# The first three blocks of a conv-and-MLP kernel in halves of 256 tokens, with the first convs mostly on TensorE

## The chip, the cores and the metric

The kernel runs on one core of one Trainium2 chip. The metric is device time in microseconds of one execution, lower is better; a time below is the median of several executions, with the lowest and highest where that matters. The changed kernel and each experiment ran on one chip together with runs of the kernel before, and are compared with those. All times that are compared are of fast runs (TensorE's mean granted clock 0.988 to 1.0); one execution in a slow state (0.563) is told apart from them. A few words used throughout: a **block** is 512 tokens of two batch rows; a **group** is the unit that the changed kernel works in, half a block or a whole one; the **first product** makes the 2048 hidden values from the conv's output, the **second product** brings them back to 192; **half clock** is said where matmuls took up to twice as long as the same ones elsewhere.

## The reference, cut to what matters

```python
# x (8, 4096, 192), weight (8 heads, 7 taps), w_in (192, 2048), w_out (2048, 192)
w = softmax(weight)                              # over the 7 taps
out[b, s, h, :] = sum_k w[h, k] * x_pad[b, s + k, h, :]     # causal conv, 6 zeros in front
h = out.reshape(32768, 192) @ w_in
y = maximum(0.01 * h, h) @ w_out                 # leaky ReLU between two products
```

## The kernel before

x is cast to bf16 and transposed by DMA, so that channels lie on partitions and tokens on the free axis (`xt`). The conv is 7 VectorE operations for each of 3 chunks of channels: one multiply and six multiply-adds (STT below) with the tap as a per-partition scalar. The first product reads the conv's result `yt`, ScalarE applies the leaky ReLU out of PSUM, and the second product of the block before is issued between the first product's steps.

```python
def conv_jobs(blk):                              # 3 chunks x 7 taps, 512 tokens each
    for c in range(NCH):
        for k in range(K):
            src = xt[rp][:, c, BASE + k + st * ST : BASE + k + (st + 1) * ST]
            # k == 0: tensor_scalar_mul(dst, src, wk[:, c, 0:1])
            # else:   scalar_tensor_tensor(out=dst, in0=src, scalar=wk[:, c, k:k+1], in1=dst, mult, add)
# ... the start
cast_first(0, 0, nc.vector.tensor_copy)
cast_first(0, 1, nc.scalar.copy)
transpose_x(0)                                   # DMA transposes, three of them
for job in conv_jobs(0):
    job()
# ... 40 matmuls that only warm TensorE up, then the loop:
for blk in range(NBLK + 1):
    jobs = conv_jobs(blk + 1) if blk + 1 < NBLK else []
    for j in range(STEPS):                       # 8 steps
        # mm1(blk, f) for two f: 12 matmuls of 512 columns, two ScalarE activations
        # mm2(n): 32 matmuls of 192 columns for the block before
        for job in jobs[3 * j : 3 * (j + 1)]:
            job()                                # next block's conv on VectorE
# ... cut: loads, softmax of the taps, output copies on VectorE
```

In the traces each engine ran its operations in the order of issue. That is what the argument below turns on: an operation that stood behind a wait waited too (VectorE's conv for 3.54 us behind one copy, under experiment 6).

## Time and profile before

| | kernel before |
|---|---|
| time, median | 715.68 us (715.51 to 715.94) |
| TensorE busy | 690.0 of 713.3 us |
| first useful matmul | 30.85 us (four of its twelve at 27.34) |
| a block in the middle | 20.93 us |
| block 4's first matmul | 109.93 us |

The lines behind this table stand in the prediction. How to read them: TensorE is busy for 97% of the span, so the middle can't get faster without less TensorE work. But the first 30.85 us hold next to no product, and the block after that has no second product to go with it. "Block 4's first matmul" is a milestone: from there on both kernels do the same, so a difference in that time is the whole difference.

### The profile page before, as it was taken

How to read it: one execution, taken by the hardware profiler on the slowest of the kernel's cores; microseconds unless marked ns; L12 is line 12 of the kernel's file. 1: busy time of each engine (PE TensorE's matmuls, PEld its weight loads, DVE VectorE, ACT ScalarE, POOL GpSimd, SP SyncE). 2: the span in 40 equal slices, each digit the busy share in tenths (PEclk: the TensorE clock that was granted, in tenths of full speed). 3: DMA queues.
4: the chain of work that ended last, by engine and by line, in shares of the span. 5: the costliest groups of instructions: out<-in, count | busy, mean ns of one | idle time of the engine just before them, and what ended most of it. 6: DMA issues, size and time to landing. Idle time of an engine off the chain costs nothing.

```text
span 713.3 us, 24704 instructions
## 1 busy us (share of the span) xinstructions
PE 690.0 (97%) x11166; PEld 593.0 (83%) x11166; DVE 535.6 (75%) x940; ACT 500.4 (70%) x518; POOL 142.0 (20%) x198
## 2 busy tenths in 40 slices
PE   2889999999999999999999999999999999999997
PEld 1347788888888888888888888888888888888887
DVE  2977877777787777788777778777777877777812
ACT  2197777777777777777777777777777777777770
POOL 7522201222210222220222222012222111000000
PEclk9999999999999999999999999999999999999999
DMA  9946435565545556653565654465556455133112
GB/s 198 152 26 79 73 77 67 76 85 79 90 66 78 75 67 90 80 75 73 79 76 73 90 81 73 74 72 76 79 80 89 66 84 72 43 69 57 46 36 67
DMA packets 188040, 55.08 MB, mean 77 GB/s; under 512 B 151584, under 2 KB 187936, under 8 KB 187936
## 3 DMA queue, kind: packets, MB, share of 16 engines
q0 software_dynamic: 98768, 14.17, 29.0%
q1 hardware_dynamic: 89152, 39.34, 24.0%
q8 instruction: 87, 1.43, 0.8%
q14 instruction: 17, 0.14, 0.1%
q10 hardware_dynamic: 16, 0.00, 0.0%
HBM read 29.88 MB, written 25.17 MB: 77 GB/s over the span
## 4 chain that ended last, share of the span: by engine, by line
PE 93%; DVE 2%; DMA 2%; ACT 2%; SPq 0%; issue 0%; DVEq 0%
PE po L248 48%; PE ph L230 45%; DVE yt L133 2%; ACT g L237 2%; DMA xt<-x_bf 1%; DMA x_nat<-in_x_dram 1%; SPq L83 0%; DVE yt L127 0%; DVE o_sb L290 0%; DVEq L127 0%
## 5 line engine op out<-in xcount | busy, mean ns | idle before, releaser
L237 ACT ACTIVATE g<-ph 128x1024 bf16<-128x1024 f32 x512 | 496.2, 1021 | 189.1 <-PE ph L230 189.1
L133 DVE SCALAR_TENSOR_TENSOR yt<-xt,wk,yt 128x512 bf16<-128x512 bf16 x576 | 431.4, 749 | 14.0
L248 PEld LDWEIGHTS <-g 64*128 64x128 bf16 (+1 forms) x8048 | 374.6, 94 | 32.7 <-issue 0.2
L230 PE MATMUL ph<-yt,w_in 64*128 64x512 bf16 x3072 | 393.8, 377 | 5.4 <-DVE yt L133 2.9
L248 PE MATMUL po<-w_out,g 64*128 64x192 bf16 (+1 forms) x8048 | 399.0, 243 | 0.0
L230 PEld LDWEIGHTS <-w_in 64*128 64x128 bf16 x3072 | 233.7, 94 | 62.8 <-issue 12.2
L74 POOL DMA_DIRECT2D x_bf<-in_x_dram x180 | 133.6, 765 | 447.4 <-DMA xt<-x_bf 437.2
L290 DVE COPY o_sb<-po 128x192 f32<-128x192 f32 x256 | 91.6, 358 | 146.6 <-PE po L248 143.9
L127 DVE TENSOR_SCALAR yt<-xt,wk 128x512 bf16<-128x512 bf16 x96 | 33.4, 348 | 9.2 <-DMA xt<-x_bf 9.2
L216 PE MATMUL warm<-xt,ident 128*128 128x512 bf16 x40 | 11.7, 466 | 10.2 <-DMA xt<-x_bf 10.2
L216 PEld LDWEIGHTS <-ident 128*128 128x128 bf16 x40 | 4.6, 115 | 16.9 <-issue 14.1
L91 ACT CAST x_bf<-x_nat 128x768 bf16<-128x768 f32 x3 | 2.5, 831 | 6.1 <-DMA x_nat<-in_x_dram 6.1
L190 PE MATMUL wps<-w,sel 8*128 8x7 f32 x6 | 1.4, 354 | 4.1 <-DVE w L187 4.1
L162 POOL DMA_DIRECT2D w_in<-in_moe_w_in_dram x8 | 5.1, 645 | 0.0
L190 PEld LDWEIGHTS wps<-w,sel 8*128 8x128 f32 x6 | 1.4, 321 | 4.0 <-issue 4.0
L170 ACT ACT_TABLE_LOAD x1 | 1.3, 1283 | 1.4 <-PEq L332 1.4
L167 POOL DMA_DIRECT2D w_out<-in_moe_w_out_dram x1 | 1.2, 1201 | 1.7 <-DMA w_in<-in_moe_w_in_dram 1.7
L196 DVE COPY wk<-wps 128x21 f32<-128x21 f32 x1 | 0.2, 181 | 1.6 <-PE wps L190 1.6
L152 POOL TENSOR_SCALAR_AFFINE_SELECT sel<-sel 8x384 f32<-8x384 f32 x2 | 1.1, 535 | 0.1
L175 DVE TENSOR_REDUCE nmax<-w 8x1 f32<-8x7 f32 x1 | 0.1, 148 | 1.2 <-DMA w<-in_weight_dram 1.2
L91 DVE CAST x_bf<-x_nat 128x768 bf16<-128x768 f32 x1 | 0.9, 941 | 0.0
L182 DVE TENSOR_REDUCE ssum<-w 8x1 f32<-8x7 f32 x1 | 0.1, 149 | 0.8 <-ACT w L179 0.8
(14 smaller groups left out, 2.7 us busy)
## 6 DMA issues: line engine op xcount, KB each, us to landing
out_dram<-o_sb SPq DMA_DIRECT2D x128, 192.0 KB, 2.1
x_bf<-in_x_dram POOLq DMA_DIRECT2D x180, 64.0 KB, 3.2
x_nat<-in_x_dram SPq DMA_DIRECT2D x4, 384.0 KB, 4.6
w_in<-in_moe_w_in_dram POOLq DMA_DIRECT2D x8, 192.0 KB, 8.7
xt<-x_bf SPq DMA_TRANSPOSE x96, 2.5
w_out<-in_moe_w_out_dram POOLq DMA_DIRECT2D x1, 768.0 KB, 15.9
w<-in_weight_dram ACTq DMA_DIRECT2D x1, 0.2 KB
```

Of the source, the lines that this page charges most:

```text
L74: nc.gpsimd.dma_start(out=t[:, c, :, e, :], in_=src[2 * rp + e, :, :, c * CH : (c + 1) * CH],)
L91: copy(out=x_bf[blk][:, :, :, e, :], in_=x_nat[blk][:, e, :, :].rearrange("p s (c k) -> p c s k", c=NCH),)
L127: lambda s=src, d=dst, c=c: nc.vector.tensor_scalar_mul(d, s, wk[:, c, 0:1])
L133: lambda s=src, d=dst, c=c, k=k: nc.vector.scalar_tensor_tensor(out=d, in0=s, scalar=wk[:, c, k : k + 1], in1=d, op0=mybir.AluOpType.mult, ...
L162: nc.gpsimd.dma_start(out=w_in[e * CH : (e + 1) * CH, :, fs], in_=moe_w_in[:, fs].rearrange("(c p) f -> p c f", p=CH),)
L170: nc.scalar.activation(out=junk, in_=junk, func=mybir.ActivationFunctionType.Exp)
L190: nc.tensor.matmul(out=wps[:, 0, c * K : (c + 1) * K], lhsT=sel[:, c, :, :].rearrange("h e k -> h (e k)"), rhs=w8, start=True, stop=True,)
L216: nc.tensor.matmul(out=wa[:, 0, :], lhsT=ident, rhs=xt[0][:, 0, HALO : HALO + ST], start=(i == 0), stop=(i == NWARM - 1),)
L230: nc.tensor.matmul(out=ph[:, e, :], lhsT=w_in[ps, c, f * 128 : (f + 1) * 128], rhs=y[ps, c, :], start=(c == 0), stop=(c == NCH - 1),)
L237: return nc.scalar.activation(out=g[blk][:, f, :, :], in_=ph, func=mybir.ActivationFunctionType.Prelu, alpha=0.01,)
L248: ins = nc.tensor.matmul(out=po[m], lhsT=g[b][ps, fc, e, s * 128 : (s + 1) * 128], rhs=w_out[ps, fc, :], start=(rt != 1 and fc == 0), stop ...
L290: nc.vector.tensor_copy(out=o_sb[:, n % 2, :], in_=po.pop(n))
```

## The change

It is meant to start the products sooner. The first three blocks are cut into halves of 256 tokens (groups 0 to 5; block 3, whole, is group 6). x of blocks 0 and 1 is transposed on TensorE, out of PSUM by VectorE and ScalarE. In groups 0 and 1 the conv of two of the three chunks is done by matmuls with diagonal matrices (one per tap, twice, as a tap is split into two bf16 parts). The output copies of the first three blocks move from VectorE to ScalarE.

```diff
+    NHALF = 3
+    NPEC = 2
+    groups = [(b, h * HT, HT) for b in range(NHALF) for h in range(2)]
+    groups += [(b, 0, ST) for b in range(NHALF, NBLK)]
...
+    def transpose_first(q):      # 12 nc.tensor.transpose of 64 x 128 into two PSUM tiles
+    def evac_first(q, *copies):  # the two copies into xt
+    def pe_conv_jobs(grp, c):    # 14 matmuls: lhsT=diag[c][:, p, k, :], rhs=xt shifted by k
...
-    transpose_x(0)
-    for job in conv_jobs(0):
-        job()
+    transpose_first(0)
+    warm(3)
+    evac_first(0, nc.vector.tensor_copy, nc.scalar.copy)
+    # diag[0] by 2 VectorE products, diag[1] by 14 ScalarE activations
+    # chunks 0, 1 by pe_conv_jobs, chunk 2 by conv_jobs
...
+        copy = nc.scalar.copy if b < NHALF else nc.vector.tensor_copy
...
+            if i in (1, 2) and j == 0:
+                transpose_first(i + 1)
+                evac_first(i + 1, nc.vector.tensor_copy, nc.vector.tensor_copy)
+            for job in ahead[per * j : per * (j + 1)]:
+                job()
+            if i == 1 and j == 3:
+                for e in range(2):
+                    cast_first(3, e, nc.vector.tensor_copy)
```

(Cut: loads in halves, the softmax's reciprocal after the matmul, the bookkeeping of second-product slots. `i` is the group, `j` its step; a half group has 4 steps, a whole one 8.)

More of the change, by code (lines that the diff above doesn't have):

```diff
@@ L38 @@
     SUB = ST // 128
+    HT = ST // 2
+    HS = SUB // 2
     NFC = F // 128
@@ L41 @@
     NBLK = (B // 2) * NB
-    STEPS = 2 * SUB
-    FPS = NFC // STEPS
     LAG = NFC + NFC // 2
-    LAST = (NBLK - 1) * STEPS - 1
     WQ = 4
+    NHALF = 3
+    NPEC = 2
     const_pool = ctx.enter_context(tc.tile_pool(name="const", bufs=1))
@@ L78, in load_x @@
         x_bf[blk] = t
-    def load_first(blk):
-        t = stage_pool.tile([128, 2, SUB, D], FP32, name="x_nat")
-        for e in range(2):
-            nc.sync.dma_start(
-                out=t[:, e, :, :],
-                in_=x[e, blk * ST : (blk + 1) * ST, :].rearrange("(c p) d -> p c d", p=128),
-            )
-        x_nat[blk] = t
-        x_bf[blk] = xb_pool.tile([128, NCH, SUB, 2, CH], BF16, name="x_bf")
-    def cast_first(blk, e, copy):
-        copy(
-            out=x_bf[blk][:, :, :, e, :],
-            in_=x_nat[blk][:, e, :, :].rearrange("p s (c k) -> p c s k", c=NCH),
-        )
     def transpose_x(blk):
@@ L101, in transpose_x @@
         if st == 0:
-            xt[rp] = xt_pool.tile([128, NCH, HALO + S], BF16, name="xt")
-            nc.vector.memset(xt[rp][:, :, 0:HALO], 0.0)
+            new_xt(rp)
         t = x_bf.pop(blk)
@@ L111, in transpose_x, with new_xt, load_first, cast_first @@
             )
+    def new_xt(rp):
+        xt[rp] = xt_pool.tile([128, NCH, HALO + S], BF16, name="xt")
+        nc.vector.memset(xt[rp][:, :, 0:HALO], 0.0)
+    def load_first(q):
+        t = stage_pool.tile([128, 2, HS, D], FP32, name="x_nat")
+        for e in range(2):
+            nc.sync.dma_start(
+                out=t[:, e, :, :],
+                in_=x[e, q * HT : (q + 1) * HT, :].rearrange("(c p) d -> p c d", p=128),
+            )
+        x_nat[q] = t
+    def cast_first(q, e, copy):
+        if q % 2 == 0 and e == 0:
+            x_bf[q // 2] = xb_pool.tile([128, NCH, SUB, 2, CH], BF16, name="x_bf")
+        h = q % 2
+        copy(
+            out=x_bf[q // 2][:, :, h * HS : (h + 1) * HS, e, :],
+            in_=x_nat[q][:, e, :, :].rearrange("p s (c k) -> p c s k", c=NCH),
+        )
@@ new lines @@
+    ptr = {}
+    def transpose_first(q):
+        ts = [
+            psum_o.tile([128, HS, NCH, CH], BF16, name=f"ptr{i}", tag="po") for i in range(2)
+        ]
+        for s in range(HS):
+            for c in range(NCH):
+                for i in range(2):
+                    ps = slice(i * CH, (i + 1) * CH)
+                    nc.tensor.transpose(
+                        out=ts[i][:, s, c, :],
+                        in_=x_bf[q // 2][ps, c, (q % 2) * HS + s, :, :].rearrange(
+                            "p e k -> p (e k)"
+                        ),
+                        identity=ident[ps, ps],
+                    )
+        ptr[q] = ts
@@ L114, with conv_jobs @@
+    def evac_first(q, *copies):
+        dst = xt[0][:, :, HALO + q * HT : HALO + (q + 1) * HT].rearrange(
+            "p c (s i k) -> p i s c k", s=HS, i=2
+        )
+        for i, t in enumerate(ptr.pop(q)):
+            copies[i](out=dst[:, i], in_=t)
     yt = {}
-    def conv_jobs(blk):
+    def conv_jobs(grp, chunks=range(NCH)):
+        blk, t0, T = grp
         rp, st = divmod(blk, NB)
-        y = yt_pool.tile([128, NCH, ST], BF16, name="yt")
-        yt[blk] = y
+        if blk not in yt:
+            yt[blk] = yt_pool.tile([128, NCH, ST], BF16, name="yt")
+        y = yt[blk]
@@ L120, in conv_jobs @@
         jobs = []
-        for c in range(NCH):
+        for c in chunks:
             for k in range(K):
-                src = xt[rp][:, c, BASE + k + st * ST : BASE + k + (st + 1) * ST]
-                dst = y[:, c, :]
+                a = BASE + k + st * ST + t0
+                src = xt[rp][:, c, a : a + T]
+                dst = y[:, c, t0 : t0 + T]
                 if k == 0:
@@ L138, in conv_jobs @@
         return jobs
+    def pe_conv_jobs(grp, c):
+        blk, t0, T = grp
+        acc = psum_o.tile([128, ST], FP32, name="acc", tag="po")
+        jobs = []
+        for k in range(K):
+            for p in range(2):
+                jobs.append(
+                    lambda k=k, p=p: nc.tensor.matmul(
+                        out=acc[:, :T], lhsT=diag[c][:, p, k, :],
+                        rhs=xt[0][:, c, BASE + k + blk * ST + t0 : BASE + k + blk * ST + t0 + T],
+                        start=(k == 0 and p == 0), stop=(k == K - 1 and p == 1),
+                    )
+                )
+        return jobs, lambda copy: copy(out=yt[blk][:, c, t0 : t0 + T], in_=acc[:, :T])
+    w9 = const_pool.tile([H, K + 1], FP32, name="w9")
+    nc.scalar.dma_start(out=w9[:, 0:K], in_=weight)
     load_first(0)
-    w8 = const_pool.tile([H, K], FP32, name="w8")
-    nc.scalar.dma_start(out=w8, in_=weight)
     load_first(1)
+    zero = const_pool.tile([128, ST], BF16, name="zero")
+    nc.vector.memset(zero, 0.0)
+    junk = const_pool.tile([128, 1], FP32)
+    nc.vector.memset(junk, 0.0)
     ident = const_pool.tile([128, 128], BF16)
@@ L167, with warm @@
     nc.gpsimd.dma_start(out=w_out, in_=moe_w_out.rearrange("(c p) d -> p c d", p=128))
-    junk = const_pool.tile([128, 1], FP32)
-    nc.vector.memset(junk, 0.0)
+    wa = psum_h.tile([128, 2, ST], FP32, name="warm", tag="ph")
+    def warm(n):
+        for _ in range(n):
+            nc.tensor.matmul(
+                out=wa[:, 0, :], lhsT=zero[:, 0:128], rhs=zero, start=True, stop=True
+            )
     nc.scalar.activation(out=junk, in_=junk, func=mybir.ActivationFunctionType.Exp)
     nmax = const_pool.tile([H, 1], FP32)
-    ssum = const_pool.tile([H, 1], FP32)
     nc.vector.tensor_reduce(
-        out=nmax, in_=w8, axis=mybir.AxisListType.X,
+        out=nmax, in_=w9[:, 0:K], axis=mybir.AxisListType.X,
         op=mybir.AluOpType.max, negate=True,
@@ L179 @@
     nc.scalar.activation(
-        out=w8, in_=w8, func=mybir.ActivationFunctionType.Exp, bias=nmax, scale=1.0,
-    )
-    nc.vector.tensor_reduce(
-        out=ssum, in_=w8, axis=mybir.AxisListType.X, op=mybir.AluOpType.add,
-    )
-    nc.vector.tensor_scalar_add(ssum, ssum, 1e-9)
-    nc.vector.reciprocal(ssum, ssum)
-    nc.vector.tensor_scalar_mul(w8, w8, ssum)
+        out=w9[:, 0:K], in_=w9[:, 0:K], func=mybir.ActivationFunctionType.Exp,
+        bias=nmax, scale=1.0, accum_out=w9[:, K : K + 1],
+    )
+    warm(6)
     wps = psum_h.tile([128, 2, ST], FP32, name="wps", tag="ph")
@@ L190 @@
         nc.tensor.matmul(
-            out=wps[:, 0, c * K : (c + 1) * K],
+            out=wps[:, 0, c * (K + 1) : (c + 1) * (K + 1)],
             lhsT=sel[:, c, :, :].rearrange("h e k -> h (e k)"),
-            rhs=w8, start=True, stop=True,
+            rhs=w9, start=True, stop=True,
         )
-    wk = const_pool.tile([128, NCH, K], FP32, name="wk")
-    nc.vector.tensor_copy(
-        out=wk, in_=wps[:, 0, 0 : NCH * K].rearrange("p (c k) -> p c k", c=NCH)
-    )
+    new_xt(0)
     cast_first(0, 0, nc.vector.tensor_copy)
@@ L202 @@
     cast_first(0, 1, nc.scalar.copy)
-    transpose_x(0)
-    for job in conv_jobs(0):
-        job()
-    cast_first(1, 0, nc.scalar.copy)
-    cast_first(1, 1, nc.scalar.copy)
-    transpose_x(1)
-    load_x(2)
-    wa = psum_h.tile([128, 2, ST], FP32, name="warm", tag="ph")
-    NWARM = 40
-    for i in range(NWARM):
-        nc.tensor.matmul(
-            out=wa[:, 0, :], lhsT=ident, rhs=xt[0][:, 0, HALO : HALO + ST],
-            start=(i == 0), stop=(i == NWARM - 1),
-        )
-    g, po, osb, seal = {}, {}, {}, {}
@@ L224, in mm1 @@
-    def mm1(blk, f):
+    wraw = wps[:, 0, 0 : NCH * (K + 1)].rearrange("p (c k) -> p c k", c=NCH)
+    rsum = const_pool.tile([128, NCH, 1], FP32)
+    nc.vector.tensor_scalar_add(rsum, wraw[:, :, K : K + 1], 1e-9)
+    nc.vector.reciprocal(rsum, rsum)
+    wk = const_pool.tile([128, NCH, K], FP32, name="wk")
+    nc.vector.tensor_mul(wk, wraw[:, :, 0:K], rsum.to_broadcast([128, NCH, K]))
+    wkb = const_pool.tile([128, NCH, K], BF16, name="wkb")
+    wkp = const_pool.tile([128, 2, NCH, K], FP32, name="wkp")
@@ new lines @@
+    nc.vector.tensor_copy(out=wkb, in_=wk)
+    nc.vector.tensor_copy(out=wkp[:, 0], in_=wkb)
+    nc.vector.tensor_sub(wkp[:, 1], wk, wkp[:, 0])
+    transpose_first(0)
+    warm(3)
+    evac_first(0, nc.vector.tensor_copy, nc.scalar.copy)
+    diag = [const_pool.tile([128, 2, K, 128], BF16, name=f"diag{c}") for c in range(NPEC)]
+    for p in range(2):
+        nc.vector.tensor_mul(
+            diag[0][:, p],
+            ident[:, None, :].to_broadcast([128, K, 128]),
+            wkp[:, p, 0, :, None].to_broadcast([128, K, 128]),
+        )
+        for k in range(K):
+            nc.scalar.activation(
+                out=diag[1][:, p, k, :], in_=ident,
+                func=mybir.ActivationFunctionType.Copy, scale=wkp[:, p, 1, k : k + 1],
+            )
@@ new lines @@
+    cast_first(1, 1, nc.scalar.copy)
+    load_first(2)
+    jobs = conv_jobs(groups[0], range(NPEC, NCH))
+    for c in range(NPEC):
+        pe_jobs, evac_y = pe_conv_jobs(groups[0], c)
+        for job in pe_jobs:
+            job()
+        if c == 0:
+            for job in jobs:
+                job()
+            evac_y(nc.vector.tensor_copy)
+        else:
+            evac_y(nc.scalar.copy)
+    cast_first(1, 0, nc.vector.tensor_copy)
+    load_first(3)
+    load_x(2)
+    transpose_x(2)
@@ L225, in mm1 @@
+    g, po, osb, seal = {}, {}, {}, {}
+    subs = [
+        (b, e, t0 // 128 + s)
+        for b, t0, T in groups for e in range(2) for s in range(T // 128)
+    ]
+    NSUB = len(subs)
+    LAST = NSUB - 2 * SUB - 1
+    unsealed = []
+    def mm1(grp, u):
+        blk, t0, T = grp
         y = yt[blk]
+        nf = ST // T
         ph = psum_h.tile([128, 2, ST], FP32, name="ph", tag="ph")
-        for c in range(NCH):
-            for e in range(2):
-                ps = slice(e * CH, (e + 1) * CH)
-                nc.tensor.matmul(
-                    out=ph[:, e, :],
-                    lhsT=w_in[ps, c, f * 128 : (f + 1) * 128],
-                    rhs=y[ps, c, :],
-                    start=(c == 0),
-                    stop=(c == NCH - 1),
-                )
@@ L237, in mm1 @@
-        return nc.scalar.activation(
-            out=g[blk][:, f, :, :], in_=ph,
+        for i in range(nf):
+            f = nf * u + i
+            for c in range(NCH):
+                for e in range(2):
+                    ps = slice(e * CH, (e + 1) * CH)
+                    nc.tensor.matmul(
+                        out=ph[:, e, i * T : (i + 1) * T],
+                        lhsT=w_in[ps, c, f * 128 : (f + 1) * 128],
+                        rhs=y[ps, c, t0 : t0 + T],
+                        start=(c == 0),
+                        stop=(c == NCH - 1),
+                    )
@@ L239, in mm1 @@
+        act = nc.scalar.activation(
+            out=g[blk][:, nf * u : nf * (u + 1), :, t0 : t0 + T],
+            in_=ph.rearrange("p e (i t) -> p i e t", i=nf),
             func=mybir.ActivationFunctionType.Prelu, alpha=0.01,
         )
+        while unsealed:
+            seal[unsealed.pop()] = act.ins.name
     def mm2_one(rt, m, fc):
-        b, jj = divmod(m, STEPS)
-        e, s = divmod(jj, SUB)
+        b, e, s = subs[m]
         if rt != 1 and fc == 0:
@@ L254, in mm2_one @@
         )
+        if rt == 0 and fc == NFC - 1:
+            unsealed.append(m)
         if rt == 1 and fc == 0:
             tc.add_manual_dep(
-                ins.ins, seal[m + 1],
+                ins.ins, seal[m],
                 mybir.DependencyInfo(
@@ L264, in mm2_one, with mm2_slot @@
             )
-    def mm2(n):
-        if n <= LAST:
-            for fc in range(NFC if n < LAST else LAG):
-                if n < LAST:
-                    mm2_one(0, n, fc)
-                t1 = n * NFC + fc - LAG
-                if t1 >= 0:
-                    mm2_one(1, *divmod(t1, NFC))
-                    if t1 % NFC == NFC - 1:
-                        evac_o(t1 // NFC)
-        if n >= LAST:
-            for fc in range(NFC):
-                mm2_one(None, n, fc)
-            evac_o(n)
+    def mm2_slot(q):
+        n, fc = divmod(q, NFC)
+        if n < LAST:
+            mm2_one(0, n, fc)
+        t1 = q - LAG
+        if t1 >= 0:
+            mm2_one(1, *divmod(t1, NFC))
+            if t1 % NFC == NFC - 1:
+                evac_o(t1 // NFC)
     def evac_o(n):
-        blk, j = divmod(n, STEPS)
-        rp, st = divmod(blk, NB)
-        e, s = divmod(j, SUB)
+        b, e, s = subs[n]
+        rp, st = divmod(b, NB)
         if n % 2 == 0:
@@ L289, in evac_o @@
         o_sb = osb[n // 2]
-        nc.vector.tensor_copy(out=o_sb[:, n % 2, :], in_=po.pop(n))
+        copy = nc.scalar.copy if b < NHALF else nc.vector.tensor_copy
+        copy(out=o_sb[:, n % 2, :], in_=po.pop(n))
         if n % 2 == 1:
@@ L296, in evac_o @@
             )
-    for blk in range(NBLK + 1):
-        if blk < NBLK:
-            g[blk] = g_pool.tile([128, NFC, 2, ST], BF16, name="g", tag="g")
-        jobs = conv_jobs(blk + 1) if blk + 1 < NBLK else []
-        for j in range(STEPS):
-            n = (blk - 1) * STEPS + j
-            if blk < NBLK:
-                for f in range(FPS * j, FPS * (j + 1)):
-                    act = mm1(blk, f)
-                    if f == FPS * j:
-                        seal[n] = act.ins.name
-            if n >= 0:
-                mm2(n)
-            if blk + 2 < NBLK:
-                if j == 2:
-                    load_x(blk + 3)
-                if j == 4:
-                    transpose_x(blk + 2)
-            for job in jobs[3 * j : 3 * (j + 1)]:
-                job()
+    slot, avail = 0, 0
@@ new lines @@
+    for i, grp in enumerate(groups):
+        blk, t0, T = grp
+        steps = T // 64
+        if t0 == 0:
+            g[blk] = g_pool.tile([128, NFC, 2, ST], BF16, name="g", tag="g")
+        quota = (avail - slot) // steps
+        if i == 0:
+            ahead, pe_ahead = [], []
+        else:
+            ahead = conv_jobs(groups[i + 1]) if i + 1 < len(groups) else []
+        per = -(-len(ahead) // (steps - 1)) if T == ST else -(-len(ahead) // steps)
+        for j in range(steps):
+            for u in range(2 * j, 2 * j + 2):
+                mm1(grp, u)
+                if i == 0 and u == 0:
+                    transpose_first(1)
+                    evac_first(1, nc.vector.tensor_copy, nc.vector.tensor_copy)
+                    ahead = conv_jobs(groups[1], range(NPEC, NCH))
+                    evacs = []
+                    for c in range(NPEC):
+                        pe_jobs, evac_y = pe_conv_jobs(groups[1], c)
+                        pe_ahead += pe_jobs
+                        evacs.append(evac_y)
+                    per = len(ahead)
+                if i == 0 and u >= 2:
+                    n = -(-len(pe_ahead) // (8 - u))
+                    for job in pe_ahead[:n]:
+                        job()
+                    pe_ahead = pe_ahead[n:]
+            for _ in range(quota):
+                mm2_slot(slot)
+                slot += 1
+            if i == 0 and j == 3:
+                for evac_y in evacs:
+                    evac_y(nc.vector.tensor_copy)
+                for e in range(2):
+                    cast_first(2, e, nc.vector.tensor_copy)
+            if i in (1, 2) and j == 0:
+                transpose_first(i + 1)
+                evac_first(i + 1, nc.vector.tensor_copy, nc.vector.tensor_copy)
+            for job in ahead[per * j : per * (j + 1)]:
+                job()
+            if i == 1 and j == 3:
+                for e in range(2):
+                    cast_first(3, e, nc.vector.tensor_copy)
+            last_half = t0 + T == ST
+            if j == steps // 4 and last_half:
+                load_x(blk + 3)
+            if j == steps // 2 and last_half and blk > 0:
+                transpose_x(blk + 2)
+        avail += 2 * T // 128 * NFC
@@ L321 @@
+    while slot < LAST * NFC + LAG:
+        mm2_slot(slot)
+        slot += 1
+    for n in range(LAST, NSUB):
+        for fc in range(NFC):
+            mm2_one(None, n, fc)
+        evac_o(n)
 _INS = ['x', 'weight', 'moe_w_in', 'moe_w_out']
```

## The prediction

> **What bounds the kernel now.** I read the page first, then the time line of the start, the table of windows and the chain of waits there. From the page:
>
> ```profile
> PE 690.0 (97%) x11166; PEld 593.0 (83%) x11166; DVE 535.6 (75%) x940; ACT 500.4 (70%) x518; POOL 142.0 (20%) x198
> PE po L248 48%; PE ph L230 45%; DVE yt L133 2%; ACT g L237 2%; DMA xt<-x_bf 1%; DMA x_nat<-in_x_dram 1%; SPq L83 0%; DVE yt L127 0%; DVE o_sb L290 0%; DVEq L127 0%
> L237 ACT ACTIVATE g<-ph 128x1024 bf16<-128x1024 f32 x512 | 496.2, 1021 | 189.1 <-PE ph L230 189.1
> L133 DVE SCALAR_TENSOR_TENSOR yt<-xt,wk,yt 128x512 bf16<-128x512 bf16 x576 | 431.4, 749 | 14.0
> L290 DVE COPY o_sb<-po 128x192 f32<-128x192 f32 x256 | 91.6, 358 | 146.6 <-PE po L248 143.9
> ```
>
> 93% of the chain is the two matmul lines: in its long middle the kernel is bound by TensorE, and the change does not touch that middle. Only the start can be worth anything, and there the time line says:
>
> ```profile
> 5.63 0.83 ACT L91 CAST x_bf<-x_nat 128x768 bf16<-128x768 f32 x1 [2.51 <-DMA x_nat<-in_x_dram]
> 6.64 24.39 SPq L106 DMA_TRANSPOSE xt<-x_bf  x9
> 15.74 0.35 DVE L127 TENSOR_SCALAR yt<-xt,wk 128x512 bf16<-128x512 bf16 x1 [9.16 <-DMA xt<-x_bf]
> 16.13 4.69 DVE L133 SCALAR_TENSOR_TENSOR yt<-xt,wk,yt 128x512 bf16<-128x512 bf16 x6
> 20.74 0.35 DVE L127 TENSOR_SCALAR yt<-xt,wk 128x512 bf16<-128x512 bf16 x1
> 30.85 1.04 PE L230 MATMUL ph<-yt,w_in 64*128 64x512 bf16 x8 [2.91 <-DVE yt L133]
> ```
>
> (Columns: start, length, engine, line, operation, count, idle before and its releaser.) x arrives by 5.6 us, the transposing DMA takes 9 us, the first conv of three chunks takes 3 x 5 us on VectorE, and the first matmul that makes headway starts at 30.85 us. Then comes a stretch in which the first block's first product has nothing to overlap with and ScalarE sets the pace: from 36.21 to 45.89 us the groups of 12 matmuls start 1.93 us apart, two activations of 0.967 us. From 49.78 us on the pattern is regular: 12 first-product matmuls, then 32 second-product ones, every 2.62 us, eight times a block:
>
> ```profile
> 89.00 1.47 PE L230 MATMUL ph<-yt,w_in 64*128 64x512 bf16 x12
> 90.30 1.54 PE L248 MATMUL po<-w_out,g 64*128 64x192 bf16 x32
> 109.93 1.50 PE L230 MATMUL ph<-yt,w_in 64*128 64x512 bf16 x12
> ```
>
> A block is 20.93 us: block 1 starts in effect at 47.2 us, blocks 2, 3, 4 at 68.1, 89.0 and 109.93 us. The two 512-token loops are alike from block 4 on, with the same second-product work (blocks 0 to 2) issued by then. So the whole change is read from one number: **when block 4's first matmul starts**, 109.93 us now.
>
> [...] after the 2.91 us wait above, pairs of weight loads stand 0.43 us apart (32.74, 33.17, 33.59, 34.02) where later ones stand 0.216, and the window 31:46 has a granted clock of 0.89. [...] The trace: 12 matmuls of 512 columns, in pairs on two row tiles, take 1.30 us, 216 ns a pair. [...]
>
> **The change: the first group.** The first load is halved, so I take casts at about 4.3 us. TensorE does 6 zero matmuls at half rate (2.6 us from 1.3), then the weight matmuls (1.42 us in the trace), to about 5.3[...]. VectorE does six small operations of about 0.19 us to 6.5, one eviction [...] to 7.1, two diagonal builds of 896 elements [...] to 9.35, then the third chunk's conv. A 256-element STT is 752 - 267 = 485 ns, 521 with the 36 ns that a dependent neighbour waits (the six above: 4.69 us = 5 x 0.788 + 0.752); the first op about 0.32. A chunk of 256 is so 0.32 + 5 x 0.521 + 0.40 = **3.33 us**, against 5.0 for 512: two halves cost a third more than a whole. That conv ends at 12.7, the eviction of chunk 0 at 13.1. Beside it ScalarE builds 14 diagonals [...] and TensorE runs 2 x 14 tap matmuls (0.11 us warm, 0.21 cold). First useful matmul: **13.3 us, 17.5 earlier**.
>
> **Group 0** does 8 activations (7.7 us) with 12 transposes and 28 tap matmuls among its matmuls. As the tap matmuls stand in TensorE's order between units that wait for ScalarE, I get about 10 us: group 1 at 23.4.
>
> **Groups 1 to 6: VectorE.** A half group of TensorE work is 48 pairs x 0.109 + 64 slots x 0.0825 = 10.5 us. VectorE now owes per half 3 x 3.33 = 10.0 us of conv[...]. And it may not start: the transposes stand after the first step's 2 units and 16 slots (2.62 us), the eviction after them, the conv after that, the next group's first product after the conv. [...]
> - Group 2 starts at 23.4 + 14.7 = 38.1 (TensorE idle 3.2).
> - Group 3 at 38.1 + 14.7 + 1.2 of half clock in the first step = 54.0 (idle some 3).
> - Groups 4, 5: TensorE and VectorE both need about 10 to 10.5; VectorE is free-running and ends their convs at 64 and 74.
> - Group 6 (block 3, whole) has a conv of 15.0 us against group 5's 10.5 of TensorE: ready at 89.0, TensorE done at 85.5, or later by what the clock costs: idle 2 to 3.5.
> - Group 6's own length: its second-product share is only one half group's (64 slots), so 10.4 + 5.3 = 15.7 on TensorE, but ScalarE has 16 x 0.967 [...]; with the hand-overs 16.7.
> - Block 4 starts at **105.7 to 106.2**, against 109.93: gain about 4 us.
>
> Sum: 715.68 - 4.0 = **711.7 us**. The same as a ledger from the first matmul to block 4: TensorE's work is 4 x 10.4 + 384 x 0.0825 = 73.3 us in both. Before, it takes 79.1 us (5.8 lost to ScalarE in block 0). After: 73.3, plus 3.0 of tap matmuls, [...] 0.9 of ScalarE in group 0, 9.9 of waits for convs, 1.2 of half clock, 1.0 of ScalarE in group 6: 92.3. So 17.5 is gained at the front and 13.2 is given back.
>
> **Rivals.**
> 1. *VectorE keeps pace.* Without its stalls: 23.4 + 11.5 + 11.5 + 3 x 10.5 + 16.6 = 94.5 at block 4, gain 15.4, 700.3 us. For it: moving output copies to ScalarE shows that this load was meant to be eased, and VectorE has 4.3 us a block to spare in the middle (16.7 of 21 busy in the window 88:109). Against: the 256-element cost above, which has only the 512-element row behind it but would need to be 0.35 us per op.
> 2. *The half clock bites at every stall.* [...] Each may cost 1.3 us (six pairs at 0.43 for 0.216) and what follows in the chain. I have counted one; three more, or a cold start of the tap matmuls (+1.5 each), make 714 to 716.
> 3. *Weights arrive late.* w_in's eight DMAs land 8.7 us (median) after issues from 2.9 to 8 us, w_out 15.9 us after 9.74, at 25.6. The second product would now want w_out at 24.7. Fewer transposing DMAs run then, so I think it lands sooner; if not, a microsecond.
>
> **Range and chances.** The first group is good to 1.5 us, the two gated groups to 1 each, group 6 to 1, and they add rather than cancel when the clock drops: 707 to 715.5 holds it 8 times in 10. Over 2% faster means under 701.4, which is rival 1 almost in full: 0.07. Slower by 2% would need 18 us of new stalls: 0.02. Within 2%: 0.91.
>
> **What would show it.** First useful matmul near 13.3 and group 1 near 23.4; a 256-element STT near 485 ns; TensorE idle for about 3 us, released by VectorE's conv, near 35 to 38 and 51 to 54, 2 to 3.5 near 87; block 4's first 12 matmuls near 106; the middle still 20.93 us a block and the tail unchanged. The prediction is wrong if STT of 256 is under 400 ns, if the transposes are released earlier than I read from the order of issue, or if a stall appears that I have no wait for (w_out, ScalarE in group 6, a PSUM buffer held by the transposes).

Where the text is cut, it told of the hardware what no run of this case shows. Its sums are left as they came out, with the cut terms in them:

- The start (first useful matmul at 13.3 us) had estimates for the twelve transposes, an eviction, the two diagonal builds and ScalarE's 14 diagonals. Measured in the changed kernel: 0.50 us at 5.31 and 0.35 at 15.07 for twelve transposes, 0.35 for an eviction on VectorE, 1.08 for a build, 4.20 for the 14 diagonals.
- The period of a gated group came to 14.7 us, and to 11.5 without the gate. In the 14.7 are the step's 2.6 and the conv's 10.0; the terms for the transposes and the evictions are cut. Measured: 0.35 us for twelve transposes at full clock, 0.62 for two evictions. The waits of 9.9 us in the ledger follow from these sums.
- ScalarE's 16.5 us in group 6 (16.7 with the hand-overs, and so the ledger's 1.0) are 16 x 0.967 and a cut term for four output copies. Measured: 0.327 us a copy.
- The ledger's 92.3 us holds a cut term for the transposes; the terms that stand come to 89.3.

Three terms that stand had no run behind them then, but the later runs show them. The 267 ns taken off the STT of 512 elements (752 ns on the mean in the kernel before): the STT of 256 takes 485 in the changed kernel. The 0.109 us a pair of 256 columns: 12 pairs take 1.31 us there (45.87 to 47.18). The taps' 0.11 and 0.21 us: 0.116 in e_hoist6_warm (27 in 3.13) and one every 0.21 in the changed kernel (9.59 to 12.79 us). The 0.0825 us a slot is 1.32 us for 16 slots in the chain of the kernel before.

## The result, and the profile after

The changed kernel takes **710.21 us** (709.95 to 711.75, 4 runs) against 715.6 for the kernel before in the same rounds: a ratio of 0.9929, 95% interval 0.9912 to 0.9947. (A ratio is the mean time of one kernel's fast runs over that of the other's in the same rounds, so not quite the ratio of the medians.) That is faster, and within the 2%.

First the page of the changed kernel: busy times, the chain that ended last, and the groups that answer to those shown of before.

```profile
PE 694.9 (98%) x11527; PEld 609.1 (86%) x11527; DVE 537.1 (76%) x970; ACT 509.2 (72%) x558; POOL 142.0 (20%) x198
PE 90%; DVE 8%; issue 1%; ACT 0%; ACTq 0%
L174 DVE SCALAR_TENSOR_TENSOR yt<-xt,wk,yt 128x512 bf16<-128x512 bf16 (+1 forms) x606 | 431.8, 713 | 15.8
L387 DVE COPY o_sb<-po 128x192 f32<-128x192 f32 x232 | 83.0, 358 | 135.2 <-PE po L348 132.6
L387 ACT COPY o_sb<-po 128x192 f32<-128x192 f32 x24 | 7.8, 327 | 0.3 <-PE po L348 0.3
L149 DVE COPY xt<-ptr 128x384 bf16<-128x384 bf16 x7 | 2.2, 352 | 7.8 <-PE ptr L135 7.8
```

VectorE's share of the chain went up from 2% to 8%, although the conv of the first block is partly gone from it: the engine that was off the path after the start is now on it for a large part of the first 90 us. The last line says what it waits for there: VectorE waited 7.8 us in all for the transposes of TensorE.

Now TensorE's time line in the changed kernel from group 1's end on, cut to the starts of groups 2, 3 and 6 and of block 4 (start, length, engine, line, operation, count, idle before and its releaser):

```profile
35.78 0.40 PE L328 MATMUL ph<-yt,w_in 64*128 64x256 bf16 x4
39.01 1.27 PE L328 MATMUL ph<-yt,w_in 64*128 64x256 bf16 x20 [2.83 <-DVE yt L174]
40.10 2.56 PE L348 MATMUL po<-w_out,g 64*128 64x192 bf16 x32
42.41 0.56 PE L135 MATMUL ptr<-ident,x_bf 64*128 64x64 bf16 x12
42.75 1.98 PE L328 MATMUL ph<-yt,w_in 64*128 64x256 bf16 x24
44.55 1.50 PE L348 MATMUL po<-w_out,g 64*128 64x192 bf16 x32
...
51.13 0.40 PE L328 MATMUL ph<-yt,w_in 64*128 64x256 bf16 x4
53.87 2.23 PE L328 MATMUL ph<-yt,w_in 64*128 64x256 bf16 x20 [2.34 <-DVE yt L174]
...
86.86 0.61 PE L328 MATMUL ph<-yt,w_in 64*128 64x512 bf16 x4
88.76 1.04 PE L328 MATMUL ph<-yt,w_in 64*128 64x512 bf16 x8 [1.29 <-DVE yt L174]
...
104.96 1.58 PE L328 MATMUL ph<-yt,w_in 64*128 64x512 bf16 x12
```

And VectorE's, over the step that leads from group 2 to group 3:

```profile
35.87 3.09 DVE L174 SCALAR_TENSOR_TENSOR yt<-xt,wk,yt 128x256 bf16<-128x256 bf16 x6
38.87 0.74 DVE L120 CAST x_bf<-x_nat 128x384 bf16<-128x384 f32 x2
42.98 0.62 DVE L149 COPY xt<-ptr 128x384 bf16<-128x384 bf16 x2 [3.36 <-PE ptr L135]
43.63 0.41 DVE L168 TENSOR_SCALAR yt<-xt,wk 128x256 bf16<-128x256 bf16 x1
44.08 3.09 DVE L174 SCALAR_TENSOR_TENSOR yt<-xt,wk,yt 128x256 bf16<-128x256 bf16 x6
```

Read the two together, they are one loop. TensorE starts four matmuls of group 2 at 35.78, with the two chunks that are ready, and then waits 2.83 us for VectorE's last STT of the conv. As soon as that is done, VectorE wants the transposes of the next half, but these stand in TensorE's order behind 24 first-product and 32 second-product matmuls; so VectorE waits 3.36 us for TensorE. Each engine waits for the other in turn. The line at 40.10 shows one more thing: 32 second-product matmuls take 2.56 us where the same 32 take 1.50 at 44.55. Just after its wait TensorE fell to half clock (granted 0.55 from 40.10 to 42.66 us, 1.00 from 44.55 to 46.05).

The milestones, before and after:

| | before | after |
|---|---|---|
| first useful matmul | 30.85 us (four of its twelve 27.34) | 14.0 (ten of its twelve matmuls 14.53) |
| block 1's start | 47.2 | 39.01 (group 2) |
| block 2's start | 68.1 | about 65.8 (group 4) |
| block 3's start | 89.0 | 88.76 past its wait (group 6) |
| block 4's start | 109.93 | 104.96 |

Counted from the matmuls behind the last wait, 16.3 us are gained at the front (30.85 less 14.53). By the clock, nearly all of it is gone at block 3's start, but the two kernels have not done the same work by then: the second product runs one group behind the first, and with half groups that lag is half a block shorter. So at 88.76 us the changed kernel is ahead by 0.2 us and by half a block of second product, 64 slots or 5.3 us at 0.0825 us a slot (1.32 us for 16 slots). Group 6 therefore takes only 16.2 us. Both kernels are level again at block 4, and of the 16.3 us some 11 were given back, nearly all before block 3. The totals differ by 5.4 us (medians) and the profiled spans by 4.7: the milestone holds the whole difference.

### The profile page after: what moved, and what is told of

Read it like the earlier page. It is cut to its first block, busy times and chain, and to the rows that moved or that the text cites. A ratio compares the mean times of both kernels' runs of the same rounds, so it can differ in the third digit from the quotient of the medians.

```text
span 708.6 us, 25496 instructions
## 1 busy us (share of the span) xinstructions
PE 694.9 (98%) x11527; PEld 609.1 (86%) x11527; DVE 537.1 (76%) x970; ACT 509.2 (72%) x558; POOL 142.0 (20%) x198
## 4 chain that ended last, share of the span: by engine, by line
PE 90%; DVE 8%; issue 1%; ACT 0%; ACTq 0%
PE po L348 45%; PE ph L328 43%; DVE yt L174 7%; PE acc L189 1%; DVE yt L168 1%; PE warm L235 0%; ACT g L335 0%; DVE xt L149 0%; PE wps L253 0%; DVE diag L280 0%; PE ptr L135 0%; DVE yt L195 0%; ACT yt L195 0%; DVE o_sb L387 0%; DVE zero L204 0%
## 5 line engine op out<-in xcount | busy, mean ns | idle before, releaser
L174 DVE SCALAR_TENSOR_TENSOR yt<-xt,wk,yt 128x512 bf16<-128x512 bf16 (+1 forms) x606 | 431.8, 713 | 15.8
L328 PE MATMUL ph<-yt,w_in 64*128 64x512 bf16 (+1 forms) x3360 | 394.7, 359 | 7.4 <-DVE yt L174 6.5
L328 PEld LDWEIGHTS <-w_in 64*128 64x128 bf16 x3360 | 244.9, 94 | 55.9 <-issue 12.1
L387 DVE COPY o_sb<-po 128x192 f32<-128x192 f32 x232 | 83.0, 358 | 135.2 <-PE po L348 132.6
L168 DVE TENSOR_SCALAR yt<-xt,wk 128x512 bf16<-128x512 bf16 (+1 forms) x101 | 34.6, 343 | 0.1
L189 PE MATMUL acc<-xt,diag 128*128 128x256 bf16 x56 | 9.6, 325 | 1.4 <-DVE diag L280 1.4
L189 PEld LDWEIGHTS <-diag 128*128 128x128 bf16 x56 | 5.8, 114 | 5.4 <-DVE diag L280 2.6
L387 ACT COPY o_sb<-po 128x192 f32<-128x192 f32 x24 | 7.8, 327 | 0.3 <-PE po L348 0.3
L235 PE MATMUL warm<-zero 128*128 128x512 bf16 x9 | 4.2, 628 | 1.3 <-DVE junk L206 1.3
L286 ACT ACTIVATE diag<-ident,wkp 128x128 bf16<-128x128 bf16 x14 | 4.2, 386 | 0.2 <-DVE wkp L271 0.2
```

The lines of the kernel that those rows point to most:

```text
L168: lambda s=src, d=dst, c=c: nc.vector.tensor_scalar_mul(d, s, wk[:, c, 0:1])
L174: lambda s=src, d=dst, c=c, k=k: nc.vector.scalar_tensor_tensor(out=d, in0=s, scalar=wk[:, c, k : k + 1], in1=d, op0=mybir.AluOpType.mult, ...
L189: lambda k=k, p=p: nc.tensor.matmul(out=acc[:, :T], lhsT=diag[c][:, p, k, :], rhs=xt[0][:, c, BASE + k + blk * ST + t0 : BASE + k + blk * ...
L235: nc.tensor.matmul(out=wa[:, 0, :], lhsT=zero[:, 0:128], rhs=zero, start=True, stop=True)
L286: nc.scalar.activation(out=diag[1][:, p, k, :], in_=ident, func=mybir.ActivationFunctionType.Copy, scale=wkp[:, p, 1, k : k + 1],)
L328: nc.tensor.matmul(out=ph[:, e, i * T : (i + 1) * T], lhsT=w_in[ps, c, f * 128 : (f + 1) * 128], rhs=y[ps, c, t0 : t0 + T], start=(c == 0) ...
```

## The experiments

**Theory.** After the start the changed kernel is set by a gate: the conv of groups 2 and 3 can begin only after the transposes, which stand behind a step of TensorE's work. Then it is set by the first whole block's conv, which needs 15 us of VectorE in a half group of 10.5 us. **Rivals.** VectorE has too much to do in halves whatever the order; or half clock after the waits is the cost; or taps and transposes cost TensorE as much as they bring.

### 1. The gate: block 1's transposes moved ahead

```diff
             if i == 0 and j == 3:
+                # casts of block 1's two halves, then the two evictions, then:
+                transpose_first(2)
+                evac_first(2, nc.vector.tensor_copy, nc.vector.tensor_copy)
-            if i in (1, 2) and j == 0:
-                transpose_first(i + 1)
-                evac_first(i + 1, nc.vector.tensor_copy, nc.vector.tensor_copy)
+            if i == 1 and j == 0:
+                transpose_first(3)
...
+            if i == 1 and j == 1:
+                evac_first(3, nc.vector.tensor_copy, nc.vector.tensor_copy)
```

> The casts and TensorE transposes of block 1 are moved ahead, so that VectorE's conv for groups 2 and 3 no longer waits for the first step of the group before. Theory (the gate costs the time, VectorE's throughput suffices in groups 2 to 5): group 2 starts at about 36.1 us instead of 39.0, group 3 at 46.6 instead of 53.9, no wait there; the wait before group 6 grows from 1.3 to about 3.2 us; block 4 starts near 97.6 instead of 104.96, so about 702.8 us (7.4 us less than the changed kernel). Rival (VectorE owes too much work in halves whatever the order): the waits reappear before the same groups, gain under 2 us.

Measured: 704.54 us (702.11 to 705.24), ratio to before 0.9841 (0.9822 to 0.986). TensorE's waits between 12 and 110 us (us in total, times, longest):

```profile
PE ph L328 <- DVE yt L174: 2.9, 1, 2.9
PE ph L328 <- ACT g L335: 0.3, 1, 0.3
PE ph L328 <- ACT yt L195: 0.2, 1, 0.2
```

The same operations, the same count, only earlier, and the waits before groups 2 and 3 are gone: they start at 36.20 and 46.95 (36.1 and 46.6 expected). One wait is left, 2.95 us before group 6, where 3.2 was expected. The rival that VectorE can't keep up in halves falls. Block 4 starts at 99.73, not 97.6, and the total is 704.5, not 702.8: half clock followed the wait that was left (the 8 matmuls after it took 1.87 us, where the changed kernel's took 1.04), and group 6 takes 17.6 us instead of 16.2. So moving the transposes ahead is worth 5 to 6 us: 5.2 by block 4's start, 5.7 by the medians (710.21 less 704.54).

### 2. The last wait: four and six blocks in halves

```diff
-    NHALF = 3
+    NHALF = 4
```

> Four blocks in halves instead of three, nothing else. Theory: VectorE needs 9.96 us a half group and TensorE 10.5, so each more half group gives the conv of the first whole block 0.55 us more lead; the wait before that block falls from 1.3 to about 0.7 us, and two more half groups cost nothing: block 5 starts near 124.9 instead of 125.9, total about 709.2 (1.0 less). Rival (halves themselves cost in every group, by more weight loads or by ScalarE taking the output copies): same or slower, 710.5 to 712.

Measured: 708.90 us (708.62 to 708.95), ratio 0.9907 (0.989 to 0.9923). Block 5 starts at 124.82 us (124.9 expected), and the wait before the first whole block is 0.73 us (0.7 expected). So two more halves cost nothing and lend VectorE the lead it lacks.

Six blocks in halves, together with experiment 1:

> Block 1's transposes ahead as in e_hoist, and six blocks in halves instead of three. Theory: each half group gains VectorE 0.56 us (9.96 against 10.52), six more are worth 3.3 us, so the 2.95 us wait before the first whole block goes to about 0.3 and the half clock after it with it: block 7 starts near 158.0 instead of 162.5, about 700.0 us. Rival (VectorE can't use the slack, as x arrives or yt comes free too late, or ScalarE's copies bind): no better than e_hoist's 704.5 by over 1 us.

Measured: 700.13 us (699.32 to 700.88), ratio 0.9786 (0.977 to 0.9802), against 700.0 expected. TensorE has no wait for VectorE's conv left at all in the first 170 us, and block 7 starts at 158.66 (158.0 expected). The theory gave both numbers before they were run, so the chain "gate, then one whole conv in half a group's time" is shown, not only argued.

### 3. The half clock: zero matmuls into the waits

```diff
+        if i in (2, 3):
+            fill = psum_h.tile([128, 2, ST], FP32, name="fill", tag="ph")
+            for _ in range(12):
+                nc.tensor.matmul(out=fill[:, 0, :], lhsT=zero[:, 0:128], rhs=zero, start=True, stop=True)
```

> The changed kernel with 12 zero matmuls of 512 columns (2.6 us) put into TensorE's waits at the start of groups 2 and 3, so that it isn't idle there and keeps its full clock; nothing it computes changes. Theory (the half clock costs 1.4 us after each wait; in group 2 it delays the transposes of group 3 and so goes through to its conv; in group 3 it is hidden, as VectorE's conv for group 6 ends last anyway): first step of groups 2 and 3 takes 2.6 us instead of 4.1, group 3 starts 1.4 to 1.7 us earlier, group 6 too: about 708.7 (1.5 less). Rival A (the clock costs in every group, 2.8 us in all): 707.4. Rival B (zero matmuls do not keep the clock up, or only move the wait): 710.2 or more.

Measured: 711.09 us (709.89 to 711.69), ratio 0.9937 (0.9924 to 0.9951): no gain; the theory's 708.7 missed, and rival B (the wait only moves) came true. TensorE's time line of this run:

```profile
34.97 2.76 PE L411 MATMUL fill<-zero 128*128 128x512 bf16 x12
37.66 1.55 PE L328 MATMUL ph<-yt,w_in 64*128 64x256 bf16 x24
39.04 1.50 PE L348 MATMUL po<-w_out,g 64*128 64x192 bf16 x32
...
48.95 2.76 PE L411 MATMUL fill<-zero 128*128 128x512 bf16 x12
51.65 1.66 PE L328 MATMUL ph<-yt,w_in 64*128 64x256 bf16 x24
...
83.38 0.61 PE L328 MATMUL ph<-yt,w_in 64*128 64x512 bf16 x4
87.02 1.89 PE L328 MATMUL ph<-yt,w_in 64*128 64x512 bf16 x8 [3.03 <-DVE yt L174]
```

The first half of the theory holds: with the filling the steps run at full clock (1.50 us for 32 second-product matmuls at 39.04, where the changed kernel took 2.56). But TensorE, no longer slowed in groups 2 and 3, reaches group 6 sooner than VectorE's conv does. It waits there for 3.03 us instead of 1.29, half clock follows (8 matmuls in 1.89 us instead of 1.04), and group 6 takes 17.4 us. Block 4 starts at 104.39 instead of 104.96, but this execution was already 0.92 us ahead at group 1 (24.29 instead of 25.21), before anything that was edited. From group 1 to block 4 it takes 80.10 us, the changed kernel 79.75. Time that is taken off an engine that then waits for another one comes back as a wait.

Two later experiments confirm this by chance. In the profile of e_dmafirst neither the wait before group 2 nor the one before group 3 was followed by half clock (32 second-product matmuls took 1.50 us after each), in that of e_notaps_again the first was not (1.50 too); yet from group 1 to block 4 they take 80.27 us (35.12 to 115.39) and 80.29 us (29.61 to 109.90). Where the gate is gone, in e_hoist, the same stretch takes 74.49. So the half clock in groups 2 and 3 is not what holds the changed kernel.

### 4. The taps on TensorE: all of the conv back on VectorE

```diff
-    NPEC = 2
+    NPEC = 0        # no diagonals, no tap matmuls; three chunks by conv_jobs in groups 0 and 1
```

> All of the first two convs back on VectorE (no diagonals, no tap matmuls), halves and TensorE transposes kept. Theory: first useful matmul at about 17.2 us instead of 14.0, group 1 at 28.7 instead of 25.2[...]: 3.5 to 5 us slower than the changed kernel, 714 to 715. Rival (the tap matmuls in group 0 cost TensorE as much as they save VectorE): within 1 us of the changed kernel.

Measured: 716.58 us median, ratio 1.0003 (0.9978 to 1.0027), so as slow as the kernel before. One of its four executions, the profiled one, took 1210.22 us at a mean clock of 0.563 (0.54 to 0.56 from 30 us to its end) and is left out of the ratio; what brought it was not shown. So the run was repeated.

> The kernel of e_notaps again, unchanged, because its profile fell into a state in which TensorE stayed at half clock for the whole run. Theory: 714 to 717 us, group 1 at about 29 us instead of 25.2, so that the tap matmuls are worth 4 to 6 us. [...]

Measured: 716.71 us (715.25 to 717.31), ratio 1.0012 (0.9998 to 1.0026). The first full step of matmuls starts at 17.47 us (17.2 expected) and group 1 at 29.61 instead of 25.21. The taps on TensorE are worth about 6 us, all of the gain of the change; without them halves and TensorE transposes bring nothing. The expectation was 1 to 2 us short: TensorE waits 3.48, 3.00, 2.92 and 2.56 us, one after the other, and group 0 ran at half clock (48 of its matmuls in a row took 4.75 us, where 24 take 1.49 at 39.01), which I had put in for one step.

### 5. The transposes of block 0 back on the DMA

```diff
     def transpose_first(q):
+        if q < 2:       # three transposing DMAs of 256 columns, no eviction
+            ...
+            return
```

(Cut: `evac_first` does nothing for these two halves, and the second half's DMAs are issued before the loop, right after its cast.)

> Block 0's two halves are transposed by the transposing DMA again instead of by TensorE; taps, halves and block 1 kept. Theory: the DMA took 9 us in the kernel before; here the transposed x comes at 11 to 13 us instead of 6.9, first useful matmul at 17 to 18.5 instead of 14.0, and the second half's transposes, which start after its cast, hold up the taps of group 1: total 3.5 to 8 us slower than the changed kernel, 714 to 718. Rival (half-size transposing DMAs are as quick as the 2.5 us of the middle of the kernel): under 1.5 us slower.

Measured: 721.35 us (720.34 to 723.33), ratio 1.0086 (1.0068 to 1.0103): slower than the kernel before. The first chunk is there at 12.26 us and the third at 15.81, against 6.9 in the changed kernel, and the first product starts at 19.61. The direction was right and the size was short (714 to 718): I had the first half's delay but not that the second half's three DMAs would land between 25 and 26 us, so that group 0 lasts 15.5 us instead of 11.2, nor that the wait before group 6 would grow to 2.94 us and be followed by half clock (12 matmuls took 2.50 us at 99.94, and 1.48 a step later).

### 6. The output copies back on VectorE

```diff
-        copy = nc.scalar.copy if b < NHALF else nc.vector.tensor_copy
+        copy = nc.vector.tensor_copy
```

> The output copies of the first three blocks go back from ScalarE to VectorE, nothing else. Theory (VectorE is what sets the end of groups 1 to 6): four copies of about 0.3 us in each half group lengthen its chain by 0.6 in group 2, 1.2 in groups 3 to 6 each: block 4 starts about 5 us later, 714 to 716, and the wait before group 6 grows. Rival (the copies fit into VectorE's gaps, as in the middle of the kernel): within 1 us of the changed kernel.

Measured: 724.04 us (723.15 to 724.82), ratio 1.012 (1.0105 to 1.0136). That is 14 us slower than the changed kernel, and 5 were expected. VectorE's time line before group 6's conv:

```profile
78.70 1.52 DVE L174 SCALAR_TENSOR_TENSOR yt<-xt,wk,yt 128x256 bf16<-128x256 bf16 x3
83.76 0.36 DVE L387 COPY o_sb<-po 128x192 f32<-128x192 f32 x1 [3.54 <-PE po L348]
84.03 0.34 DVE L168 TENSOR_SCALAR yt<-xt,wk 128x512 bf16<-128x512 bf16 x1
```

The copies take 0.35 us each, near the 0.3 expected. But a copy has to wait for its second product, and everything behind it in VectorE's order waits too. VectorE has done group 5's conv at 80.2 us and could begin the long conv of the whole block; it stands for 3.54 us because the copy in front is not ready. VectorE stands 13.4 us in all before these copies, and their own time is 7.4 us. TensorE then waits 17.2 us in all for the conv (6.5 in the changed kernel), 4.73 of it before group 6. So moving the copies to ScalarE does two things: it takes load off VectorE, and it cuts VectorE loose from TensorE, so that it can run ahead. My expectation held only the first. How the 14 us divide between the two was not tested.

The runs also show that the length of a wait alone does not decide whether half clock follows it. Before group 2, e_dmafirst and e_warm both waited 2.69 us. First e_dmafirst, then e_warm:

```profile
48.78 1.27 PE L341 MATMUL ph<-yt,w_in 64*128 64x256 bf16 x20 [2.69 <-DVE yt L186]
49.87 1.50 PE L361 MATMUL po<-w_out,g 64*128 64x192 bf16 x32
```

```profile
37.19 1.27 PE L328 MATMUL ph<-yt,w_in 64*128 64x256 bf16 x20 [2.69 <-DVE yt L174]
38.27 2.62 PE L348 MATMUL po<-w_out,g 64*128 64x192 bf16 x32
```

After the same wait the 32 second-product matmuls ran at full clock in one and at half in the other. The 32 took 1.50 us after waits of 2.80 us (e_dmafirst, before group 3) and of 3.17 us (e_evacdve, before group 3) too, but 2.56 after the 2.83 us of the changed kernel. What decides was not shown.

### 7. The first taps at full clock, and the fastest version

In the changed kernel the taps of group 0 begin at half clock, by their pace of one every 0.21 us: all 27 take 5.09 us, 0.19 us each. Four more zero matmuls ahead of them should keep TensorE busy until the diagonals are built.

```diff
     transpose_first(0)
-    warm(3)
+    warm(7)
```

> e_hoist6 with 7 zero matmuls instead of 3 after the first transposes, so that TensorE is busy until the first diagonals are there. Theory: the tap matmuls of group 0 ran 0.21 us apart until about 11.7 us and closer after, that is at half clock; at full clock from the start they end by about 12 and the first useful matmul comes at about 13.0 instead of 14.5: 1.2 to 1.7 us less than e_hoist6. Rival (the clock comes up no sooner, and the four more zero matmuls delay the taps by up to 0.7 us): same or 0.7 us more.

Measured, on top of experiments 1 and 2: **698.95 us** (698.59 to 699.3), ratio 0.9768 (0.9754 to 0.9781). Taps and first product of this run:

```profile
8.98 3.13 PE L189 MATMUL acc<-xt,diag 128*128 128x256 bf16 x27 [0.24 <-DVE diag L280]
13.28 0.83 PE L328 MATMUL ph<-yt,w_in 64*128 64x256 bf16 x12 [1.16 <-DVE yt L195]
```

27 tap matmuls take 3.13 us instead of 5.09 (5.94 in the profile of e_hoist6), and the first useful matmul comes at 13.28. The total is 1.2 us under e_hoist6, at the low end of what was expected. What the first product waits for is now VectorE's part (1.16 us), so more warming should bring nothing; that was not tried. This version beats both kernels. The outputs are right.

> The changed kernel with 7 zero matmuls instead of 3 after the first transposes, alone, without the moved transposes and with three blocks in halves. Theory: the first useful matmul comes about 1.3 us earlier, as in e_hoist6_warm, and all of it passes through to block 4, since every group from 1 to 3 is chained to the one before: about 709 us, and with less spread than the changed kernel's 1.8 us. Rival (the waits in groups 2, 3 and 6 swallow it): 710.2.

Alone on the changed kernel: 709.30 us (708.74 to 711.12), ratio 0.992 (0.9904 to 0.9935), an interval that overlaps the changed kernel's. In the profiled run block 4 starts at 103.41 (1.55 us earlier), but the spread did not shrink. Whether the 0.9 us is real can't be told from these runs.

All runs side by side, as ratio to the kernel before in the same rounds:

| run | median us | ratio | waits of TensorE for the conv of groups 2, 3, first whole block |
|---|---|---|---|
| the changed kernel | 710.21 | 0.9929 | 2.83, 2.34, 1.29 |
| e_hoist | 704.54 | 0.9841 | none, none, 2.95 |
| e_halves4 | 708.90 | 0.9907 | 2.69, 2.73, 0.73 |
| e_hoist6 | 700.13 | 0.9786 | none |
| e_hoist6_warm | 698.95 | 0.9768 | none |
| e_warm | 709.30 | 0.9920 | 2.69, 2.39, 1.52 |
| e_fill | 711.09 | 0.9937 | filled, filled, 3.03 |
| e_notaps, again | 716.58, 716.71 | 1.0003, 1.0012 | 2.69, 2.80, 1.28 (again), and four before |
| e_dmafirst | 721.35 | 1.0086 | 2.69, 2.80, 2.94 |
| e_evacdve | 724.04 | 1.0120 | 17.2 in all |

## Why the prediction was right

711.7 us was predicted, 710.21 measured, in the range of 707 to 715.5, and within 2% as 0.91 had it. The chain was right too (first product sooner, then two gated groups, then one whole conv in half a group's time), and its steps can be checked one by one:

| step, as predicted | predicted | measured |
|---|---|---|
| first useful matmul | 13.3 us | 14.0 to 14.53 |
| STT of 256 elements | 485 ns | 485 ns |
| chunk of 256 tokens on VectorE | 3.33 us | 3.32 (32.09 to 35.41) |
| group 1's start | 23.4 | 25.21 |
| period of groups 1, 2 | 14.7, 15.9 | 13.8, 14.9 |
| wait before groups 2, 3 | 3.2, "some 3" | 2.83, 2.34 |
| group 3's start | 54.0 | 53.87 |
| wait before group 6, its start | 2 to 3.5, 89.0 | 1.29, 88.76 |
| length of group 6 | 16.7 | 16.2 |
| block 4's start | 105.7 to 106.2 | 104.96 |

The step that carried it is the cost of a small operation, split from one row of the profile into a part per element, which no trace had shown then, and a fixed part. The two forms in the changed kernel, between 10 and 110 us (busy us, mean ns):

```profile
L174 DVE SCALAR_TENSOR_TENSOR yt<-xt,wk,yt 128x256 bf16<-128x256 bf16 x83 | 40.2, 485 | 3.0
L174 DVE SCALAR_TENSOR_TENSOR yt<-xt,wk,yt 128x512 bf16<-128x512 bf16 x41 | 30.8, 752 | 1.5
```

Half the elements take 64% of the time; by these two means 218 ns are fixed and 1.04 ns go to each element. That is why halves load VectorE more, and with the order of issue it gives the waits.

That the number fits so well is partly luck, for several sizes were off and nearly cancelled. Group 1 started 1.8 us later than predicted: the taps of group 0 ran at half clock, 0.19 us each (named under rival 2, but not in the sum), and in group 0 each unit of twelve matmuls with its five taps took 1.41 us. On the other side the periods of groups 1 and 2 were 0.9 and 1.0 us shorter: 12 transposes take 0.35 us at full clock and the two evictions 0.62 (a bf16 copy of 384 elements out of PSUM takes 352 ns on the mean), both less than I had put in, with no run behind it.

The prediction's ledger shows the same. It had 17.5 us gained at the front and 19.0 us of added cost, of which the 5.8 us lost before in block 0 pay a part. Measured, the gain is 16.3 and the added cost 17.1 (90.4 us from 14.53 to 104.96, less 73.3 of work). The waits were 6.5 us instead of 9.9, and the transposes about 1, less than the term that is cut. The half clock, though, cost about 1.6 us in each of groups 2 and 3, some 3.2 instead of the 1.2 counted, and group 0 lost some 2 us besides its taps and transposes instead of 0.9. The taps' 3.0 was right. (The sizes given with "about" or "some" are estimates, from the time line less the same matmuls at full clock.)

Of the rivals, the first (VectorE keeps pace) is wrong for the changed kernel, but VectorE's throughput does suffice: once the transposes stand earlier and VectorE has lead enough, the time is 700.13, and the prediction had 700.3 for that case. This agreement is partly luck, as six blocks in halves were not what it was worked out for. The second (the half clock bites at every stall) is half right. It did bite in the taps of group 0 and after the waits before groups 2 and 3, and not after the 1.29 us before group 6 (granted 1.00 from 88.76 to 92.00 us; what decides was not shown, see experiment 6); but experiment 3 shows that taking it away after the two waits only moves the wait on. The third (weights come late) did not show: no wait of TensorE names them.

What the prediction did not see is in the experiments: how much the move of the output copies to ScalarE is worth (14 us, where the load alone had been put at 5), and that taps and transposes on TensorE each decide between a gain and none.

## What to carry to other kernels

Cutting the first tiles in halves brings the first product forward, but it loads the engine that feeds it more, by the fixed part of each operation (here 218 of the 485 ns of an STT of 256 elements); work out that engine's time per half against the bound engine's before choosing how many halves, and give it lead before the first whole tile. Put small jobs that another engine needs (transposes, copies) ahead in the order of the busy engine, not after its next step: here that alone was worth 5 to 6 us, as much as the whole change. And an engine that is meant to run ahead must not have operations in its order that wait for the engine it runs ahead of.
